# Later transposes, stores and inverse in the second block of a two-layer H3/MLP kernel, and row statistics moved in its last units

## The chip, the cores and the metric

The kernel runs on 1 core of a Trainium2 chip. The metric is device time in microseconds (us) from one launch, median of several runs; lower is better. In the tables PE is TensorE, DVE is VectorE, ACT is ScalarE, POOL is GpSimd, and SP is SyncE, whose queue issues all the DMAs of this kernel.

## What is computed

Sequence 2048 tokens, model width 1024, hidden width 3584, float32. Two layers, each of a convolution part A and an MLP part B, with the same weights in both layers:

```python
def A(q, k, v, shift_k, ssm_k, ssm_D):
    kv = causal_conv4(k, shift_k) * v                 # per channel, 4 taps
    y = causal_conv_2048(kv, ssm_k) + kv * ssm_D      # per channel, long
    return q * y
def B(x):
    return square(relu(x @ w1 + b1)) @ w2 + b2

x = q
x = x + A(layernorm(x), ...);  x = x + B(layernorm(x))
x = x + A(layernorm(x), ...);  x = x + B(layernorm(x))
```

The long convolution does not depend on x, so it is computed once (as transforms, products and inverse transforms) and used in both layers.

## The kernel before

**Units and steps.** The tokens are cut into four blocks of 512. A unit is the MLP of one layer on one block. `ORDER` lists the eight units as (layer, block): (0,0), (1,0), (0,1), (0,2), (1,1), (0,3), (1,2), (1,3). Each unit is a list of steps; one step multiplies with one 128x1024 or 512-wide slice of `w1` (kind `m1`) or `w2` (`m2`). All of it runs in a split form: each operand is a high part plus a low part, and `mm3` (L334 to L337) issues three matmuls for each product. A full `m1` or `m2` step is 12 matmuls. Units 5, 6 and 7 (`WINO`) use a seven-product scheme for the second matrix: their steps are `m1` (12 matmuls) and `w2` (6 matmuls), in four chunks; the first two chunks are 12 `m1` steps and 21 `w2` steps each, so the second chunk's `w2` steps are steps 45 to 65 of a unit of 154. Unit 0 has a special end: its last chunk's `m2` steps (106 to 133) and unit 1's first `m1` steps (134 to 157) handle half of the tokens each, so that the next unit's input can be made between them; a step there is half as long.

**Weights.** `w_advance` runs ahead of the step: it issues loads up to 8 weights ahead on SP's queue (`w_load`), ACT makes the high part (L1012), DVE or POOL the low part (L1020). The low part of a weight is put into DVE's queue three steps before it is used. Some weights are reloaded already split (`whl<-wd_m`, L1010).

**The convolution** goes on beside the MLP steps. Block 0's is made in a prologue. For the blocks sb = 1 to 3 two generators run, `fwd_x` (transforms of k and v, 8 groups of 128 channels for each block) and `fwd_g` (transforms of the filter). A call of `next` on both is an advance. The main loop gives them `FWD_RATE` advances a step (1.4 in units 0 to 2, none in half steps), and one more for a step in which the product generator `prod_stream` has nothing to do. `yield` ends what one advance does, so the number of yields sets how far apart two instructions stand in the program. `fwd_x` computes the shifted product on DVE (L365, L367), waits some advances, transposes it on TensorE (`transposes`, L420), multiplies with the transform tables (L391), adds and subtracts on DVE and stores to `XD` (L412). `fwd_g` loads filter rows and a carried part `KD` (L427, L436), multiplies (L454), copies (L459), stores the next carried part `KD` (L463), combines on DVE (L464 to L484) and stores `GD` (L493). Both use two PSUM banks `pt`, taken with `hold` or `take` and returned with `give`.

`prod_stream` loads `XD` and `GD` (L625), multiplies on POOL (L525), reduces on DVE (L529) and, through a list of delayed calls `lag`, runs `fin`: fold and butterfly on POOL (L675, L679), then for sb <= `PLAIN` = 1 `fin_plain`: inverse transform on TensorE (L595), copy on ACT (L601), store (L606). Its speed is `pace[u]`, the work of blocks 1 and 2 divided by the steps of units 0 to 2 (324.4 after a deduction) less `PACE_SLACK[1]`. In half steps the pace is a tenth.

**Row statistics.** `prep_a` makes the layernorm statistics of the next unit's input: it loads four 128x1024 row tiles `px` (L725; the pool has two buffers), runs two `bn_stats` (L696) and one `bn_aggr` (L697) on DVE for each, three steps apart, then the reciprocal root. It starts at step 28 of a unit, and what it makes is used from the step with 90 left. In `WINO` units `b2` is loaded at step 33 into the same pool `px` (L1737) and added to eight accumulator tiles on POOL from step 37 on (`add_b2w`, L1599).

Each engine and SP's queue work in program order.

Of the kernel before, what the change touches and what calls it, by code (L numbers as in the profile page):

```python
# [22 lines left out]
NB = S // T  # L23
# [4 lines left out]
BL = 256  # L28
NBL = S // BL
BT = T // BL  # L30
# [14 lines left out]
AHEAD_0 = 4  # L45
BURST = 1.06
FIN = "GGG"
PACE_SLACK = {1: 74, 3: 10}
PACE_TO = {1: 2}
PLAIN = 1  # L50
FILL = (16, 12, 8)
# [189 lines left out]
def tile_h3_mlp(ctx: ExitStack, tc: tile.TileContext, q, kT, vT, shk, ssmT, ssmD, w1, b1, w2, b2,  # L241
# [111 lines left out]
    def fwd_x(sb, c):  # L353
        k4 = mkfx([P, T + 3])
        SY.dma_start(k4, kT[c * P:(c + 1) * P, sb * T:sb * T + T + 3])
        v4 = mkfx([P, T])
        SY.dma_start(v4, vT[c * P:(c + 1) * P, sb * T:(sb + 1) * T])
        for _ in range(FWD_WAIT):
            yield
        ks = mkfx([P, T])  # L360
        w = shkt[:, c]
        A.activation(ks, k4[:, 3:], AF.Copy, scale=w[:, 0:1])
        yield
        for s in range(1, 4):
            V.scalar_tensor_tensor(ks, k4[:, 3 - s:T + 3 - s], w[:, s:s + 1], ks, op0=OP.mult, op1=OP.add)  # L365
        yield
        V.tensor_mul(ks, ks, v4)  # L367
        for _ in range(4 if sb == 1 else 7):
            yield
        o, = yield from hold(1)  # L370
        transposes(o, ks)
        yield
        if sb <= PLAIN:
            xt = mkfx([P, T])
            A.copy(xt, o)
        else:
            hi = mkfx([P, T], F32R)
            lo = mkfx([P, T], F32R)
            A.copy(hi, o)
            yield  # L380
            V.tensor_sub(lo, o, hi.bitcast(F32))
        yield
        give(o)
        yield
        oa = yield from hold(2)
        for e in range(2):
            for r in range(2):
                q_ = slice(e * 256, e * 256 + 256)
                ou = oa[e][:, r * 256:r * 256 + 256]
                if sb <= PLAIN:  # L390
                    PE.matmul(ou, plain[0][:, 2 * e + r], xt[:, q_], start=True, stop=True)  # L391
                else:
                    mm3(ou, fh[:, 2 * e + r], fl[:, 2 * e + r], hi[:, q_], lo[:, q_], True, True)
        yield
        odd = mkfx([P, T])
        A.copy(odd, oa[1])
        yield
        xo = cv.tile([P, 2, T], F32, name="fy", bufs=1)
        xv = xo.rearrange("p r (n u c) -> p u (r n) c", u=2, c=CG)
        ev = oa[0].rearrange("p (n c) -> p n c", c=CG)  # L400
        ov = odd.rearrange("p (n c) -> p n c", c=CG)
        V.tensor_add(xv[:, 0], ev, ov)
        V.tensor_sub(xv[:, 1], ev, ov)
        yield
        give(*oa)
        x2 = mkfx([P, T])
        V.tensor_add(x2, xo[:, 0], xo[:, 1])
        yield
        yield
        for i in range(3):  # L410
            t = x2 if i == 2 else xo[:, i]
            SY.dma_start(dview(XD[i], sb, c), t.rearrange("p (g b u) -> p g b u", g=2, b=BT))  # L412
        yield
# [15 lines left out]
    def fwd_g(sb, c):  # L429
        yield  # L430
        yield
        raw = mkfg([P, T])
        load_g(raw, sb, c)
        kk = [mkfk([P, 3 * BL]) for _ in range(2)]
        for r in range(2):
            SY.dma_start(kk[r][:, 0:BL], KD[sb - 1][c][:, r])  # L436
        for _ in range(FWD_WAIT):
            yield
        if sb > PLAIN:
            hi = mkfg([P, T], F32R)  # L440
            lo = mkfg([P, T], F32R)
            A.copy(hi, raw)
            yield
            V.tensor_sub(lo, raw, hi.bitcast(F32))
            yield
            yield
            yield
        oa = yield from hold(2)
        for r in range(2):
            ob = oa[r].rearrange("p (b e c) -> p e b c", b=BT, e=2)  # L450
            for e in range(2):
                q_ = slice(e * 256, e * 256 + 256)
                if sb <= PLAIN:
                    PE.matmul(ob[:, e], plain[0][:, 2 * e + r], raw[:, q_], start=True, stop=True)  # L454
                else:
                    mm3(ob[:, e], fh[:, 2 * e + r], fl[:, 2 * e + r], hi[:, q_], lo[:, q_], True, True)
        yield
        for r in range(2):
            A.copy(kk[r][:, BL:], oa[r])  # L459
        yield  # L460
        if sb < NB - 1:
            for r in range(2):
                SY.dma_start(KD[sb][c][:, r], kk[r][:, BT * BL:])  # L463
        V.scalar_tensor_tensor(kk[1][:, 0:T], kk[1][:, 0:T], sgn[:, 1:2], oa[0], op0=OP.mult, op1=OP.add)  # L464
        V.scalar_tensor_tensor(oa[1], kk[0][:, 0:T], sgn[:, 0:1], oa[1], op0=OP.mult, op1=OP.add)
        yield
        k0 = kk[1][:, 0:T]
        V.scalar_tensor_tensor(oa[0], oa[1], -1.0, k0, op0=OP.mult, op1=OP.subtract)
        V.tensor_sub(oa[1], oa[1], k0)
        yield  # L470
        odd = mkfg([P, T])
        parts = [t.rearrange("p (b e n) -> p e b n", b=BT, e=2) for t in (k0, oa[1], oa[0])]
        odds = [parts[0][:, 1]]
        for i in range(2):
            odds.append(odd[:, i * BL:i * BL + BL].rearrange("p (b n) -> p b n", b=BT))
            A.copy(odds[-1], parts[i + 1][:, 1])
        yield
        go = [None] * 3
        for i in (1, 2, 0):
            go[i] = mkfg([P, T])  # L480
            u = go[i].rearrange("p (g b u c) -> p u b g c", g=2, b=BT, u=2)
            ev, ov = (t.rearrange("p b (g c) -> p b g c", g=2) for t in (parts[i][:, 0], odds[i]))
            V.tensor_add(u[:, 0], ev, ov)
            V.tensor_sub(u[:, 1], ev, ov)  # L484
            yield
        if sb <= PLAIN:
            yield
            yield
        give(*oa)
        yield  # L490
        yield
        for i in range(3):
            SY.dma_start(dview(GD[i], sb, c), go[i].rearrange("p (g b u) -> p g b u", g=2, b=BT))  # L493
        yield
# [24 lines left out]
    def prod_stream():  # L519
# [11 lines left out]
        def fin(st, sm, sb, g, k):  # L531
# [4 lines left out]
                lag.at(1, fin, st, sm, sb, g, 1)  # L536
            elif k == 1 and sb <= PLAIN:
                st["z"] = butterfly(E, s)
                lag.at(2, fin_plain, st, sb, g, 0)
            elif k == 1:  # L540
                pair = st["pair"]
                if "l" not in pair if g % 2 else inv[1] < inv[0]:
# [1235 lines left out]
    for s, (k, u, c, a, i, tts, w) in enumerate(steps):  # L1778
# [109 lines left out]
            early.append(load_y(b, HALF[0]))  # L1888
        if u + 1 < NU and not direct[u]:
            n = s - start_step[u]  # L1890
            if n == 28:
                pa = prep_a(*ORDER[u + 1])
            elif n > 28 and pa is not None and next(pa, 0) == 0:
                pa = None
            if u in WINO and left == W_PREP:
                nxt = prep_w(*ORDER[u + 1], lag)
            elif u not in WINO and left == 18:
                while pa is not None:
                    if next(pa, 0) == 0:
                        pa = None  # L1900
                close_conv(ORDER[u + 1][1])
                nxt = prep_b(*ORDER[u + 1], lag)
# [77 lines left out]
```

## Time and profile before

| | |
|---|---|
| median of 3 runs | 2731.35 us (2731.30 to 2731.46) |
| the profiled execution | 2731.19 us |
| its span, first to last instruction | 2729.4 us |
| PE busy | 2683.3 us (98%) |
| DVE busy | 1989.7 us (73%) |
| ACT busy | 1124.2 us (41%) |
| POOL busy | 843.9 us (31%) |
| mean granted TensorE clock | 0.998 of full speed |

Busy time is the union of an engine's instructions. PE's instructions are pipelined and overlap, so what matters is the time in which PE has none, and the distance between the starts of two matmuls.

### The profile page before, as it was taken

To read this page: it belongs to the slowest core of one execution; us is meant where nothing else is said; L and a number is where in the kernel's file an instruction comes from. 1 tells how busy PE (TensorE), PEld (TensorE's weight loads), DVE (VectorE), ACT (ScalarE), POOL (GpSimd) and SP (SyncE) were. 2 spreads that over 40 slices of the span, in tenths; PEclk is the share of its full clock that TensorE was granted. 3 is DMA by queue.
4 is the path that set the end of the run, shared out by engine and by line. 5 is a ranking of instruction groups with operands and counts; after the bars stand their busy time and mean duration, and the time that the engine had idled before them with its cause. 6 is when DMAs were issued, how large, how long until landed. Compare 5 with 4: busy or idle time off the path is not lost.

```text
span 2729.4 us, 36532 instructions
## 1 busy us (share of the span) xinstructions
PE 2683.3 (98%) x12568; PEld 2228.9 (82%) x12568; DVE 1989.7 (73%) x3066; ACT 1124.2 (41%) x1936; POOL 843.9 (31%) x532
## 2 busy tenths in 40 slices
PE   7999999999999999999999999999999999999999
PEld 6888787888888888888888888888788788888887
DVE  7878888788987877779677665366787666664555
ACT  4454344433444233442234422244455444445443
POOL 2336565345532655236543454000100010001000
PEclk9999999999999999999999999999999999999999
DMA  8789898699989898888977887688888866676545
GB/s 253 262 301 316 285 312 285 221 312 369 324 298 324 295 338 280 267 332 284 349 263 269 301 295 253 226 288 311 300 284 295 281 229 211 229 276 200 178 166 204
DMA packets 377482, 755.05 MB, mean 277 GB/s; under 512 B 43840, under 2 KB 159184, under 8 KB 377296
## 3 DMA queue, kind: packets, MB, share of 16 engines
q1 hardware_dynamic: 377296, 752.72, 80.6%
q8 instruction: 99, 1.62, 0.2%
q14 instruction: 87, 0.71, 0.1%
HBM read 602.63 MB, written 149.95 MB: 276 GB/s over the span
## 4 chain that ended last, share of the span: by engine, by line
PE 84%; DVE 6%; DMA 5%; issue 1%; POOL 1%; ACT 1%; SPq 1%; DVEq 0%; ACTq 0%; POOLq 0%
PE p L336 26%; PE p L335 26%; PE p L337 26%; DMA wr<-w 2%; PE p L1095 2%; DVE whl L1020 1%; PE pt L335 1%; PE pt L337 1%; PE pt L336 1%; DMA whl<-wd_m 1%; DVE sm L529 0%; DMA cx<-xd 0%; PE pt L391 0%; DMA cg<-gd 0%; PE p L789 0%
## 5 line engine op out<-in xcount | busy, mean ns | idle before, releaser
L525 POOL TENSOR_TENSOR cp<-cx,cg 128x384 f32<-128x384 f32 (+5 forms) x288 | 541.8, 1893 | 580.3 <-DVE sm L529 388.1
L335 PE MATMUL p<-xh,whl 128*128 128x512 f32 (+1 forms) x1840 | 706.6, 384 | 3.3 <-DMA whl<-wd_m 2.5
L337 PE MATMUL p<-xh,whl 128*128 128x512 f32 (+1 forms) x1840 | 703.6, 382 | 3.6 <-DVE whl L1020 2.8
L336 PE MATMUL p<-xl,whl 128*128 128x512 f32 (+1 forms) x1840 | 702.8, 382 | 0.1
L1012 ACT CAST whl<-wr 128x512 fp32r<-128x512 f32 x637 | 383.5, 619 | 441.6 <-PE p L337 262.4
L1020 DVE TENSOR_TENSOR whl<-wr,whl 128x512 fp32r<-128x512 f32 x622 | 500.4, 825 | 78.4 <-ACT whl L1012 73.2
L335 PE MATMUL p<-whl,rh 128*128 128x512 f32 x1372 | 548.1, 399 | 3.7 <-ACT whl L1012 2.4
L336 PE MATMUL p<-whl,rh 128*128 128x512 f32 x1372 | 543.7, 396 | 1.9 <-POOL whl L1020 1.7
L337 PE MATMUL p<-whl,rl 128*128 128x512 f32 x1372 | 542.6, 396 | 0.0
L337 PEld LDWEIGHTS p<-xh,whl 128*128 128x128 f32 x1840 | 345.9, 188 | 71.7 <-DVE whl L1020 3.0
L335 PEld LDWEIGHTS p<-xh,whl 128*128 128x128 f32 x1840 | 346.2, 188 | 70.5 <-DMA whl<-wd_m 2.6
L336 PEld LDWEIGHTS p<-xl,whl 128*128 128x128 f32 x1840 | 346.0, 188 | 66.1 <-DVE xl L1408 0.3
L335 PEld LDWEIGHTS p<-whl,rh 128*128 128x128 f32 x1372 | 259.5, 189 | 64.0 <-ACT whl L1012 3.9
L336 PEld LDWEIGHTS p<-whl,rh 128*128 128x128 f32 x1372 | 259.5, 189 | 61.9 <-POOL whl L1020 2.6
L337 PEld LDWEIGHTS p<-whl,rl 128*128 128x128 f32 x1372 | 259.4, 189 | 60.6
L1502 DVE TENSOR_TENSOR rl<-wr,rh 128x512 fp32r<-128x512 f32 x140 | 141.1, 1009 | 182.8 <-ACT rh L1497 182.7
L1599 POOL TENSOR_TENSOR acc<-acc,px 128x512 f32<-128x512 f32 x18 | 23.1, 1317 | 771.0 <-DMA px<-b 771.0
L529 DVE TENSOR_REDUCE sm<-cp 128x128 f32<-128x384 f32 (+5 forms) x288 | 249.3, 874 | 9.2 <-POOL cp L525 9.2
L1494 ACT ACTIVATE wr<-p,b1t 128x512 f32<-128x512 f32 x138 | 95.2, 690 | 379.1 <-PE p L337 375.3
L1563 DVE TENSOR_TENSOR rl<-wr,rh 128x256 fp32r<-128x256 f32 x84 | 49.8, 593 | 208.5 <-ACT rh L1558 208.4
L1622 DVE TENSOR_TENSOR acc<-p,acc 128x512 f32<-128x512 f32 x152 | 101.5, 687 | 87.3 <-PE p L337 86.9
L1555 ACT ACTIVATE wr<-p,b1t 128x512 f32<-128x512 f32 x84 | 57.9, 689 | 190.4 <-PE p L337 188.9
(277 smaller groups left out, 3310.9 us busy)
## 6 DMA issues: line engine op xcount, KB each, us to landing
whl<-wd_m SPq DMA_DIRECT2D x379, 512.0 KB, 5.1
wr<-w SPq DMA_DIRECT2D x493, 256.0 KB, 5.4
wr<-td SPq DMA_DIRECT2D x152, 256.0 KB, 4.1
wd_m<-whl SPq DMA_DIRECT2D x70, 512.0 KB, 6.0
cx<-xd SPq DMA_DIRECT2D x48, 512.0 KB, 5.7
cg<-gd SPq DMA_DIRECT2D x48, 512.0 KB, 6.4
gd<-fg SPq DMA_DIRECT2D x72, 256.0 KB, 6.2
cx<-xd SPq DMA_DIRECT2D x48, 384.0 KB, 5.8
```

Source lines behind the costliest of these rows:

```text
L335: PE.matmul(o, lh, rh, start=start, stop=False)
L336: PE.matmul(o, lh, rl, start=False, stop=False)
L337: PE.matmul(o, ll, rh, start=False, stop=stop)
L525: G.tensor_mul(pr.rearrange("p c i -> p i c"), xt[:, 0:j + 1], gt[:, j::-1])
L529: V.tensor_reduce(sm[:, ty, jj], st["pr"], axis=AX.X, op=OP.add)
L1012: A.copy(t[:, 0], raws[n]["t"])
L1020: ENG[e[n % len(e)]].tensor_sub(t[:, 1], raws[n]["t"], t[:, 0].bitcast(F32))
L1095: PE.matmul(o, lh, r, start=start, stop=stop)
L1494: A.activation(r, st["o"], AF.Relu, bias=b1t[:, st["f"]:st["f"] + 1])
L1502: V.tensor_sub(st["lo"], st["r"]["t"], st["hi"].bitcast(F32))
L1555: A.activation(r, st["o"], AF.Relu, bias=b1t[:, st["f"]:st["f"] + 1])
L1622: V.tensor_add(accs[tt][:, d], o, accs[tt][:, d])
```

## The change

Five edits. (1) `fwd_x`: for block 1 the transposes come 7 advances after the product instead of 4, as for the other blocks. (2) `fwd_g`: the store of `KD` moves from right behind the copies to behind the return of the PSUM banks; the store of `GD` comes 4 advances later than that return for block 1 instead of 2 (2 still for the other blocks). (3) The inverse of block 1 is called 3 instead of 2 ticks of `lag` after the butterfly. (4) `PACE_SLACK[1]` is 76 instead of 74. (5) In units 5 and 6 `prep_a` starts at step 45 instead of 28.

```diff
-PACE_SLACK = {1: 74, 3: 10}
+PACE_SLACK = {1: 76, 3: 10}
...
         V.tensor_mul(ks, ks, v4)
-        for _ in range(4 if sb == 1 else 7):
+        for _ in range(7):
             yield
         o, = yield from hold(1)
         transposes(o, ks)
...
             A.copy(kk[r][:, BL:], oa[r])
         yield
-        if sb < NB - 1:
-            for r in range(2):
-                SY.dma_start(KD[sb][c][:, r], kk[r][:, BT * BL:])
...
         give(*oa)
-        yield
-        yield
+        if sb < NB - 1:
+            for r in range(2):
+                SY.dma_start(KD[sb][c][:, r], kk[r][:, BT * BL:])
+        for _ in range(4 if sb <= PLAIN else 2):
+            yield
         for i in range(3):
             SY.dma_start(dview(GD[i], sb, c), go[i].rearrange("p (g b u) -> p g b u", g=2, b=BT))
...
                 st["z"] = butterfly(E, s)
-                lag.at(2, fin_plain, st, sb, g, 0)
+                lag.at(3, fin_plain, st, sb, g, 0)
...
             n = s - start_step[u]
-            if n == 28:
+            at = 45 if u in WINO else 28
+            if n == at:
                 pa = prep_a(*ORDER[u + 1])
-            elif n > 28 and pa is not None and next(pa, 0) == 0:
+            elif n > at and pa is not None and next(pa, 0) == 0:
                 pa = None
```

## Rows read from the trace of the kernel before

**Rows 1.** The page, part 1: busy us, share of the span, instructions.
```profile
PE 2683.3 (98%) x12568; PEld 2228.9 (82%) x12568; DVE 1989.7 (73%) x3066; ACT 1124.2 (41%) x1936; POOL 843.9 (31%) x532
```
**Rows 2.** Waits of PE: us in total, times, longest.
```profile
PE p L420 <- DVE fx L1134: 13.5, 3, 9.4
PE pt L420 <- DVE fx L367: 6.9, 3, 6.0
PE p L335 <- DMA whl<-wd_m: 3.6, 4, 2.2
...
PE pt L595 <- DVE fg L484: 2.0, 1, 2.0
```
**Rows 3.** Windows: length; PE, PEld, DVE, ACT, POOL busy; clock; DMA.
```profile
294.00:306.00 12.00, 5.97 (x21) 4.83 (x20) 11.66 (x16) 1.51 (x4) 8.42 (x8) 0.72 0.87 268
...
440.00:470.00 30.00, 25.89 (x114) 20.74 (x113) 22.82 (x35) 13.65 (x24) 15.49 (x11) 0.94 0.75 242
470.00:546.00 76.00, 70.83 (x460) 63.08 (x459) 59.20 (x105) 35.70 (x60) 26.05 (x17) 1.00 0.67 239
546.00:820.00 274.00, 272.63 (x1294) 227.51 (x1294) 236.51 (x320) 111.72 (x202) 137.08 (x85) 1.00 0.94 325
```
**Rows 4.** Timeline of DVE, 276 to 304 us: start, length, instruction.
```profile
291.96 0.41 DVE L484 TENSOR_TENSOR fg<-pt,fg 128x256 f32<-128x256 f32 x1
...
297.03 1.49 DVE L484 TENSOR_TENSOR fg<-fk 128x256 f32<-128x256 f32 x1
298.44 1.48 DVE L1020 TENSOR_TENSOR whl<-wr,whl 128x512 fp32r<-128x512 f32 x1
299.84 0.68 DVE L367 TENSOR_TENSOR fx<-fx 128x512 f32<-128x512 f32 x1
```
**Rows 5.** Timeline of PE, 292 to 307 us.
```profile
304.55 0.63 PE L336 MATMUL p<-whl,rh 128*128 128x512 f32 x1
304.97 0.63 PE L337 MATMUL p<-whl,rl 128*128 128x512 f32 x1
```
**Rows 6.** Waits of SP's queue, whole span: us, times, longest.
```profile
SPq L493 <- DVE fg L484: 36.6, 13, 8.8
...
SPq L463 <- ACT fk L459: 19.4, 11, 6.9
...
SPq L725 <- POOL fk L1599: 18.4, 2, 9.6
```
**Rows 7.** Timeline of SP, 438 to 475 us.
```profile
450.06 1.44 SPq L493 DMA_DIRECT2D gd<-fg  x3
...
460.74 1.52 SPq L1004 DMA_DIRECT2D wr<-w  x3
```
**Rows 8.** Timeline of DVE in unit 5, 1890 to 1930 us.
```profile
1902.77 1.29 DVE L696 BATCH_NORM_STATS2 st<-px 128x6 f32<-128x512 f32 x2 [0.43 <-DMA px<-x]
...
1904.21 1.24 DVE L1606 TENSOR_TENSOR acc<-p,acc 128x512 f32<-128x512 f32 x2
```
**Rows 9.** Timeline of DVE in unit 5, 1936 to 1972 us.
```profile
1960.32 1.39 DVE L1606 TENSOR_TENSOR fx<-p,fx 128x512 f32<-128x512 f32 x2 [0.23 <-PE p L337]
1961.63 0.68 DVE L1020 TENSOR_TENSOR whl<-wr,whl 128x512 fp32r<-128x512 f32 x1
```
**Rows 10.** Timeline of DVE in unit 6, 2238 to 2268 us.
```profile
2251.56 1.39 DVE L1606 TENSOR_TENSOR fx<-p,fx 128x512 f32<-128x512 f32 x2 [0.62 <-PE p L337]
...
2255.78 1.39 DVE L1606 TENSOR_TENSOR fx<-p,fx 128x512 f32<-128x512 f32 x2 [1.03 <-PE p L337]
2257.09 1.89 DVE L1020 TENSOR_TENSOR whl<-wr,whl 128x512 fp32r<-128x512 f32 x3
```
**Rows 11.** Timeline of PE, unit 5, step 63 of the unit.
```profile
1965.04 0.39 PE L335 MATMUL p<-whl,cg 128*128 128x512 f32 x1
1965.27 0.40 PE L336 MATMUL p<-whl,cg 128*128 128x512 f32 x1
```
**Rows 12.** Timeline of PE, unit 6, step 63 of the unit.
```profile
2260.73 0.40 PE L336 MATMUL p<-whl,cg 128*128 128x512 f32 x1
```

## The prediction

> **What bounds the kernel now.** I read the page first: PE is busy 2683.3 us of 2729.4 and the next engine, DVE, 1989.7 [rows 1]. So PE sets the time, and a change that leaves its matmuls as they are, as this one does, can win or lose only the 46 us in which PE has nothing, and what a lowered clock costs behind a long gap. Next, who PE waits for [rows 2]. The 13.5 us for L1134 are the prologue, which no edit touches. Within reach are the transposes of `fwd_x` waiting for DVE's product (L367): 6.9 us in three waits, one of them 6.0; the inverse (L595) waiting for a bank that DVE still reads: 2.0; and reloaded weights (`whl<-wd_m`): 3.6, the longest 2.2. Third, the windows, to see where the gaps lie [rows 3]: 294 to 306 us has 6.0 idle and a granted clock of 0.72; 440 to 470 has 4.1 idle and 0.94; the half steps, 470 to 546, have 5.2 idle; the 274 us behind them only 1.4, although DVE is busy 236.5 of them. Last, the queues: SP stood 36.6 us for the stores of `GD`, 19.4 for those of `KD`, and 18.4, in two waits of up to 9.6, before a load of `px` for POOL's addition of `b2` [rows 6].
>
> **The transposes (edit 1).** At 294.6 PE came to the transposes, and DVE executed the product they need at 299.84 to 300.5 [rows 4]: the 6.0 us. The next 12 matmuls then stood 0.42 us apart [rows 5] where a full-clock pair is 0.23 apart [rows 11]; that is the clock's lower level, 1.2 GHz, after 6 us without work, and costs 12 x 0.19 = 2.3. With the other two waits (0.9) this edit has 9.2 us to win. It will not win all. Three more advances at 1.4 a step are about two steps, 2 x 12 x 0.23 = 5.5 us. Instead of waiting, PE would do two steps first, and the second needs the low part of a weight that DVE made at 298.44 to 299.92, just before the product [rows 4]. PE would ask for it at 294.6 + 2.8 + 0.2 = 297.6, so 2.3 us of the wait go over to the weight. I take 9.2 - 2.3 = **-6.9**; bounds 0 (DVE later still) and -9.2.
>
> **What moves with it.** A group of `fwd_x` now takes 3 more advances, one of `fwd_g` 2. Over eight groups that is up to 24 advances, at 1.4 a step 17 steps (48 us); advances given while the product generator is idle make it fewer. The work is the same, only stretched, so DVE is less dense up to step 106 and what is left is done after the half steps, at the same rates; there DVE is already at 86% with 1.4 us idle on PE [rows 3], so I cost it at nothing, and at 2 us (another wait of the size of L595's) as the upper bound. Since alignments of DVE, ACT and SP all shift, I put those **+2** into the sum for a new wait somewhere in units 0 and 1.
>
> **The stores (edit 2).** SP's waits cost PE nothing while weights are ahead. At one place they do: SP stood up to 8.8 us until 450.06 for a `GD` store and had a backlog until 460.74, when it came back to the weights [rows 6, 7]; PE then ran dry in the window 440 to 470, which holds 4.1 idle, the inverse's 2.0 among them, and about 2 more at the lower clock (0.94) [rows 3]. The store is one of block 2's first group, for which the delay stays 2 advances; but that group now comes some 10 to 17 steps later, where the half steps stop the streams. So this stall of 6.1 either goes or turns up elsewhere: I take half, **-3**; bounds 0 and -6.1. The other `KD` and `GD` waits are hidden by weights loaded up to 8 steps ahead, and moving them wins nothing.
>
> **Inverse and pace (edits 3, 4).** The wait of L595 is in the stall just counted; other inverses never waited, so one tick more is nothing unless the product generator, which lets two groups be open, idles for it: it then hands its turn to the transforms. The pace rises by 2/248, 0.8%: nothing.
>
> **The row statistics (edit 5).** In unit 5 SP stood at the third `px` load until POOL had added `b2`; it could not issue the reloaded weights queued behind, and PE waited 2.2 us [rows 2, 6], with the restart 2.3. In unit 6 SP waited 9.6 and PE not at all. With `prep_a` at step 45, `b2` has left `px` before the tiles are asked for, so **-2.3**. But where does DVE now do it? From `bn_stats` to the next instruction one tile takes 1904.21 - 1902.77 = 1.44 [rows 8], four take 5.8. Before, they stood among `m1` steps, many of whose weights come already split. Now they stand behind steps 49, 52, 55 and 58, in a stretch of `w2` steps of 6 x 0.23 = 1.4 us, each of which needs a low part (0.6) from DVE, and evictions besides. At step 63 of unit 5 the low part was done at 1962.31 and needed at 1965.27 [rows 9, 11]: 2.96 ahead. All four tiles stand before it: 5.76, less 0.23 that DVE idled [rows 9], less 2.96, leaves **+2.6** on PE. In unit 6 the same part was done at 2257.77 and needed at 2260.73 [rows 10, 12], 2.96 again, with 0.62 + 1.03 idle on DVE ahead of it: 5.76 - 1.65 - 2.96 = **+1.15**. No other step of the stretch comes out worse. The bounds: nothing, if DVE's queue has more slack than its order shows, to the whole 5.8 in each unit. The four loads of `px` now share the queue with the `w2` weights; at worst that is once more a wait for a weight of 2.2 [rows 2], and I take nothing, since these weights are asked for 8 steps ahead. Edit 5 comes to **+1.5**.
>
> **Sum.** 2731.2 (this execution: span and 1.8 around it) - 6.9 - 3 + 2 + 1.5 = 2724.8; the median of the runs is 0.2 above the execution: **2725**.
>
> A rule that speaks against edit 1: the Trainium skill, page "SBUF — State Buffer", section "Who interferes with whom", says that a DVE instruction with two SBUF inputs and a GpSimd instruction that reads SBUF exclude each other for a whole instruction. The trace agrees: L484 took 1.49 us from SBUF alone and 0.41 with one input in PSUM [rows 4]. By that rule DVE's lateness comes from POOL's products and goes with them, and the sum would be that of the first rival.
>
> **Rivals.**
> *The wait only changes hands.* DVE is late at 294 us because its instructions took two to three times as long (1.48 for a low part against 0.68 at other places [rows 4, 9]) while POOL was busy 8.4 of 12 us [rows 3]. If POOL's products and this lateness come again beside each later transposes, PE waits for weights instead: half of 6.9 is won, the stall at 440 to 470 is replaced, and -3.4 + 2 + 1.5 gives 2731. For it: the low part stands right before the product in DVE's queue. Against: less is asked of DVE in each step before the half steps.
> *Everything clears.* -9.2 - 6.1 - 2.3, no new wait, statistics hidden: 2714. For it: DVE's waits on its own inputs leave holes. Against: the 2.96 us of lead.
> *The streams are caught at step 106 (slower).* There the program takes both `pt` banks, and makes advances on the spot until they are free. If `fwd_x` then stands between its product and its matmuls, these follow with no steps between them: a wait like the one removed, 8.3 with the clock, and one of 2.0 for a copy. -6.9 + 10.3 + 2 + 1.5 = +6.9: 2738. It decides if the generator holds or wants banks just then; before, block 2's first group already stood there, and 24 advances shift what stands there by an unknown part of a group of 22.
>
> **How the numbers follow.** No change, as far as this kernel can be measured, is within 0.2%, 5.5 us: 2725.9 to 2736.8. The forecast has 0.62, the first rival 0.17, the second 0.10, the third 0.11. The forecast's own range, from its bounds, is 2719 to 2730; seven tenths of it lie below 2725.9. Faster: 0.43 + 0.10 = 0.53. Same: 0.19 and the first rival, 0.36. Slower: 0.11. The range 2714.5 to 2733 takes in the first rival and most of the second and leaves out the third.
>
> **What would show it.** In the changed profile: PE's wait at L420 for L367 below 1 us in all, and in its place up to 2.3 for `whl` L1020; no window before 440 us with a clock near 0.7; the long stand of SP for L493 no longer within 20 us of the half steps; PE's wait for `whl<-wd_m` in unit 5 gone and SP's for L725 on POOL too; in units 5 and 6, in the second chunk's `w2` steps, PE waiting for L1020, 2.6 and 1.2 us. The prediction is wrong if L420 still waits, if half steps lose more than 8 us, or if the statistics cost nothing or more than 6.

## The result, and the profile after

The changed kernel takes **2744.6 us** (median of 6 runs, 2739.9 to 2747.0), the kernel before 2731.3 beside it (6 runs): ratio 1.0046, 95% interval 1.0033 to 1.0059. It is slower by 0.46%. I had forecast 2725, range 2714.5 to 2733. The profiled execution took 2744.4 (before 2731.2), its span 2742.6 (before 2729.4).

The page of the kernel after, part 1, against [rows 1]:
```profile
PE 2689.8 (98%) x12568; PEld 2229.5 (81%) x12568; DVE 1980.7 (72%) x3066; ACT 1124.6 (41%) x1936; POOL 835.4 (30%) x532
```
PE's time without work grew from 46.1 to 52.8 us, half of the 13.2, and the same 12568 matmuls keep PE busy 6.5 us longer. About half of these 6.5 is the clock: by the clock records of the two traces it stood at its lower level, 1.2 GHz, for 17.1 us in all instead of 10.2, which at half speed costs about 3.4 us (an estimate). Where the rest lies was not traced. What PE waits for in the kernel after (total, times, longest), against [rows 2]:
```profile
PE p L336 <- DVE whl L1020: 8.8, 10, 3.8
PE p L335 <- DMA whl<-wd_m: 6.2, 5, 3.7
PE pt L336 <- DVE yl L561: 3.0, 2, 2.0
```
The 6.9 us for L367 have no row any more; nor has L595. In their place stand low parts that DVE makes, those of weights (L1020) and of the inverse's input (L561). Waits for reloaded weights (`whl<-wd_m`) have grown from 3.6 [rows 2]. Windows of the kernel after (length; PE, PEld, DVE, ACT, POOL busy; clock; DMA), against [rows 3]:
```profile
294.00:306.00 12.00, 12.00 (x57) 9.89 (x56) 11.61 (x18) 3.63 (x7) 7.75 (x7) 1.00 1.04 387
306.00:440.00 134.00, 134.00 (x625) 111.75 (x624) 115.80 (x171) 61.27 (x111) 81.03 (x65) 1.00 0.88 290
440.00:470.00 30.00, 24.53 (x99) 18.58 (x98) 28.17 (x36) 9.99 (x17) 17.07 (x14) 0.94 0.95 351
...
546.00:820.00 274.00, 268.52 (x1260) 222.46 (x1259) 235.15 (x321) 109.16 (x199) 127.82 (x81) 0.99 0.93 322
640.00:650.00 10.00, 6.96 (x29) 5.44 (x28) 10.00 (x12) 1.83 (x3) 5.67 (x3) 0.84 1.05 355
915.00:930.00 15.00, 11.32 (x38) 8.71 (x37) 15.00 (x21) 2.59 (x5) 7.22 (x5) 0.77 1.03 345
```
From 294 to 440 us PE has no idle time left, more than I hoped for. Behind it PE is idle in places that were full: 5.5 us in 546 to 820, where it was 1.4, with the clock at 0.84 of full speed in one stretch and 0.77 in a later one. DVE is busy for 235.2 us of that window, as much as before (236.5 [rows 3]). The kernel after is 16 us ahead at 440 us, so a window there holds later steps than the same window of the kernel before.

Steps can be found in both traces by their first matmul, so each program step's start tells where time comes and goes. Steps are counted through the whole program: 106 is the first half step of unit 0, 594 begins unit 5, 639 is that unit's step 45. Differences to the kernel before, in the profiled executions (the last column is the ratio of the runs to those of the kernel before beside them, with its 95% interval):

| kernel | ahead (-) at step 106 | 106 to 594 | 594 to 639 | 639 to end | span | ratio of runs |
|---|---|---|---|---|---|---|
| after | -16.0 | +25.5 | -2.6 | +6.3 | +13.2 | 1.0046 [1.0033, 1.0059] |
| e1: edit 5 alone | -0.4 | +1.5 | -2.6 | +4.3 | +2.8 | 1.0005 [0.9996, 1.0014] |
| e2: after without edit 5 | -16.0 | +21.4 | +4.1 | +1.3 | +10.8 | 1.0048 [1.0031, 1.0065] |
| e3: edit 1 alone | -11.9 | +34.8 | -0.2 | +0.9 | +23.7 | 1.0085 [1.0070, 1.0101] |
| e17: edit 2 alone | +0.1 | +33.5 | +0.3 | +1.5 | +35.4 | 1.0131 [1.0114, 1.0148] |
| e18: edit 3 alone | +0.9 | +9.4 | +0.0 | +0.6 | +11.0 | 1.0043 [1.0028, 1.0058] |
| e7: edit 4 alone | -1.9 | +4.8 | +4.0 | +0.8 | +7.7 | 1.0041 [1.0025, 1.0057] |
| e8: after without edit 1 | -9.7 | +25.7 | -2.6 | +6.2 | +19.6 | 1.0071 [1.0054, 1.0088] |
| e10: after without edit 4 | -16.0 | +31.4 | -2.6 | +5.4 | +18.2 | 1.0064 [1.0047, 1.0081] |

So the change wins 16.0 us before the half steps and gives back 25.5 in units 0 to 4 behind them; 3.7 are lost in the last units. In the kernel after the 25.5 lie at few places: steps 106 to 120 (4.1), 134 to 158 (3.0), 190 to 194 (8.0), 278 to 282 (6.7; a reloaded weight comes 3.7 us late at 921 us), the rest in smaller ones.

Two things have to be known to read these differences. First, they hold matmuls that moved as well as waits. At step 106 the kernel after has done 24 convolution matmuls fewer, about 2.8 us of work (an estimate from the distances of such matmuls, 0.11 to 0.12 us), so that much of the 16.0 is only put off and comes back in the 25.5. At steps 190 to 194 PE idles 3.0 us and the clock takes about 1.6 (0.84 over 10 us); most of the rest of the 8.0 is matmuls that stood in neighbouring steps before. Free of this is PE's time without work between steps 106 and 594: 8.9 us before, 23.1 after. Second, two executions of one program differ. After and e2 have the same program up to unit 5; PE idles 23.1 and 22.6 us in steps 106 to 594, but the clock was low for 17.1 and 6.8 us, and they lose 25.5 and 21.4. A difference of some 4 us in that column therefore says little.

### The profile page after: what moved, and what is told of

Read it like the earlier page. It is cut to its first block, busy times and chain, and to the rows that moved or that the text cites. A ratio compares the mean times of both kernels' runs of the same rounds, so it can differ in the third digit from the quotient of the medians.

```text
span 2742.6 us, 36481 instructions
## 1 busy us (share of the span) xinstructions
PE 2689.8 (98%) x12568; PEld 2229.5 (81%) x12568; DVE 1980.7 (72%) x3066; ACT 1124.6 (41%) x1936; POOL 835.4 (30%) x532
## 4 chain that ended last, share of the span: by engine, by line
PE 82%; DMA 7%; DVE 6%; issue 2%; POOL 1%; ACT 1%; SPq 1%; DVEq 0%; POOLq 0%; ACTq 0%
PE p L336 25%; PE p L335 25%; PE p L337 25%; DMA cg<-gd 2%; PE p L1095 1%; DMA wr<-w 1%; DVE whl L1020 1%; DMA whl<-wd_m 1%; PE pt L337 1%; PE pt L336 1%; PE pt L335 1%; POOL cp L525 1%; PE pt L454 0%; DMA wd_t<-whl 0%; PE p L789 0%
## 5 line engine op out<-in xcount | busy, mean ns | idle before, releaser
L525 POOL TENSOR_TENSOR cp<-cx,cg 128x384 f32<-128x384 f32 (+5 forms) x288 | 535.9, 1876 | 608.0 <-DVE sm L529 306.5
L1020 DVE TENSOR_TENSOR whl<-wr,whl 128x512 fp32r<-128x512 f32 x622 | 499.8, 824 | 62.5 <-ACT whl L1012 59.7
L529 DVE TENSOR_REDUCE sm<-cp 128x128 f32<-128x384 f32 (+5 forms) x288 | 250.3, 875 | 47.6 <-POOL cp L525 47.6
L1502 DVE TENSOR_TENSOR rl<-wr,rh 128x512 fp32r<-128x512 f32 x140 | 147.4, 1053 | 171.0 <-ACT rh L1497 170.8
L1599 POOL TENSOR_TENSOR acc<-acc,px 128x512 f32<-128x512 f32 x18 | 23.1, 1318 | 779.5 <-DMA px<-b 779.5
```

What stands on the lines that cost most here:

```text
L525: G.tensor_mul(pr.rearrange("p c i -> p i c"), xt[:, 0:j + 1], gt[:, j::-1])
L529: V.tensor_reduce(sm[:, ty, jj], st["pr"], axis=AX.X, op=OP.add)
L1020: ENG[e[n % len(e)]].tensor_sub(t[:, 1], raws[n]["t"], t[:, 0].bitcast(F32))
L1502: V.tensor_sub(st["lo"], st["r"]["t"], st["hi"].bitcast(F32))
```

## The experiments

**Which edit? Edit 5 alone (e1) and the rest without it (e2).** e1 is the kernel before with edit 5, e2 the kernel after without it.

> The kernel before with edit 5 alone (row statistics of units 5 and 6 start at step 45). Up to step 621 its program is the kernel before's. Theory A (the loss of the change lies before unit 5; edit 5 costs DVE time in the w2 steps): the 2.3 us wait for the reloaded weights in unit 5 goes, the w2 steps 45 to 65 get 4 us longer in unit 5 and 0.8 in unit 6: +2 to +3 us on the kernel before. Theory B (edit 5 is what makes the change slower): +10 or more.

> The changed kernel without edit 5 (edits 1 to 4 alone). Theory A: the changed kernel's time less 2.5, so about +10 us on the kernel before, with the same losses in units 1 and 2 (8 us at steps 190 to 194, 7 us at steps 278 to 282). Theory B: 0 to -5 us on the kernel before.

e1 took 2732.5, no change that can be measured; without edit 5 the rest loses as much as with it (e2: 2743.2). In e1's trace the wait of unit 5 goes (-2.45 in the unit's steps 39 to 41), 2.4 come back in the `w2` steps of unit 5 and 0.8 in those of unit 6. The loss lies in the edits to the convolution, as theory A expected of both runs (e1 is 1.4 us behind where it expected 2 to 3). Among the other edits, edit 5 even wins a little: behind step 594 the kernel after loses 3.7 and e2 5.4, in one execution each.

**Edit 1 alone (e3) and everything else (e8).** e3 is the kernel before with edit 1, e8 the kernel after without it.

> The kernel before with edit 1 alone (transposes 7 advances behind the product for block 1). Theory A (stretching the second block's transforms pushes products and transforms past step 106, where they collide): about 10 us won up to step 106 and most of it or more lost behind, +3 to +12 us in all. Theory C (the losses behind step 106 are accidents of how the streams fall against the steps, so each variant has its own): the win up to step 106 is there, the losses at steps 190 and 278 are not, and the total lies anywhere from -12 to +12.

> The changed kernel without edit 1 (transposes 4 advances behind the product; the stores, the inverse, the pace and the row statistics as changed). Theory A: fwd_g alone takes 21 advances instead of 19, so there is about two thirds of the lateness; the 6 us wait of the transposes stays or moves; +5 to +15 us on the kernel before. If edit 1 alone makes the lateness: within 5 us.

e3 took 2754.6, e8 2751.0. e3 wins 11.9 up to step 106 and then loses 34.8, more than all edits together. Without edit 1 the others lose 25.7 of their own in the same stretch. The edits don't add up: alone, edits 1 to 4 cost 23.7, 35.4, 11.0 and 7.7 of span. Both runs lie above every range I had given, e3 23.4 us and e8 17.0 behind the kernel before.

**The pace: alone (e7), taken back (e10), to the other side (e11).** e7 has `PACE_SLACK[1]` 76 in the kernel before, e11 has 72 there; e10 is the kernel after with 74.

> The kernel before with edit 4 alone (slack 76 instead of 74: products 0.8% faster in units 0 to 2). Theory A: nothing, within 3 us of the kernel before. Theory C (accidents of alignment make up the loss): a shift as small as this moves single waits by 5 us or more, and the total by up to 10 either way.

> The changed kernel with PACE_SLACK[1] back at 74, so edits 1, 2, 3 and 5 without the higher pace. The pace alone cost about 10 us in the medians when put into the kernel before (5.7 in its profiled execution up to the end of unit 2 and in unit 5). If the pace's loss is a cost of its own that adds: 2734 to 2738, and steps 190 to 282 lose less. Theory C (no cost adds, each order has losses of its own): its losses stand at other steps than those of the changed kernel, with a total that can't be told from the parts, 2735 to 2760; at steps 106 it is still 14 to 16 us ahead of the kernel before, because edit 1 has acted there already.

> The kernel before with PACE_SLACK[1] 72 instead of 74: the pace of the products 0.8% lower instead of 0.8% higher, nothing else. If a higher pace costs because DVE and POOL get more work in each step, a lower pace costs nothing or wins: 2729 to 2732. Theory C (74 is matched to the rest of the order, so a step to either side loses): slower, 2735 to 2750, with new waits of 2 to 4 us of PE for DVE's low parts or for reloaded weights at single places of units 0 to 2.

0.8% more pace costs 0.41% (e7: 2744.1), 0.8% less costs 0.39% (e11: 2742.2, ratio 1.0039 [1.0024, 1.0054]), and with the old pace the kernel after is no better (2748.8). It isn't the load that a higher pace brings, since a lower one costs as much. The value 74 fits this order of the program, and a step to either side costs some 10 us. All three runs are as theory C, that the order is matched as a whole, expected.

**Are the streams late at step 106, and is that the cause? (e4, e5, e6)** In the kernel after, 83 products are done when step 106 begins, in the kernel before 90 (counted from L525's instructions), and seven more go through in the first half steps. e4 is the kernel after, with the products in half steps held to a tenth of the pace even when they are behind; e5 the kernel after with `FWD_RATE` 1.6 for unit 0, which brings the transforms back to where they were; e6 the kernel before with 1.2, which delays them.
```diff
-FWD_RATE = {0: 1.4, 1: 1.4, 2: 1.4, 3: 1.1, 4: 1.1, 5: 1}
+FWD_RATE = {0: 1.6, 1: 1.4, 2: 1.4, 3: 1.1, 4: 1.1, 5: 1}
```


> The changed kernel, with products in the half steps held to a tenth of the pace even when the product stream is in arrears (in the changed kernel arrears let through one product at nearly each half step: 7 in steps 106 to 120 where the kernel before had 1). Theory A: the 4 us that steps 106 to 120 lose go, and the products are made after step 158 instead, 2738 to 2743 in all, with the losses at steps 190 and 278 as before or larger. Theory C: the losses behind step 158 change their place and size, so that the total may lie anywhere from -10 to +15 on the kernel before.

> The changed kernel with 1.6 advances a step in unit 0 instead of 1.4, which makes up for the longer generators (22 advances a group instead of 19). Theory A (what is lost behind step 106 is lost because fewer transforms and products are done before it): the number of products at step 106 is again near 90, block 2's first transposes come before step 106, the losses at steps 106 to 120, 190 and 278 shrink; about -10 us on the kernel before. Theory C (accidents of alignment): the products at step 106 rise too, but there are losses of 5 to 10 us somewhere in units 1 and 2 all the same; anywhere from -10 to +15.

> The kernel before with 1.2 advances a step in unit 0 instead of 1.4: the second block's transforms come as late as in the changed kernel, but no distance between two instructions changes. Theory A: the loss of the changed kernel without its win, +15 to +30 us. If the longer distances, not the lateness, cost behind step 106: within 5 us of the kernel before.

e4 took 2740.6 (1.0030 [1.0017, 1.0043]): steps 106 to 120 lose 0.9 instead of 4.1, but 20.7 are lost up to step 594. e5 took 2761.0 (1.0107 [1.0092, 1.0123]), although it had 86 products done at step 106; e6 2767.6 (1.0130 [1.0115, 1.0145]). e4 is where either theory put it. e6 agrees with theory A (33.6 us behind, for 15 to 30 expected), but a lower rate also changes which instructions meet, so it doesn't show that lateness by itself costs. e5 was to win 10 us by theory A and loses 27, more than theory C allowed: making up for most of the lateness doesn't help. My first theory, that the work pushed behind step 106 is the whole cause, falls.

**Repair one wait where it stands (e9).** At 644 us PE waits 2.0 for the inverse's low part and drops to the lower clock. e9 is the kernel after with
```diff
                 if g % 2:
-                    lag.at(1, fin, st, sm, sb, g, 4)
+                    lag.at(2, fin, st, sm, sb, g, 4)
```


> The changed kernel, with the inverse transforms of blocks 2 and 3 called 2 ticks behind the low part yl instead of 1; nothing else. In the changed kernel PE waits 3.0 us in two waits for yl, one of 2.0 at 644 us, and steps 190 to 194 take 8.0 us longer than before. Theory A2 (each loss is PE meeting, in program order, an instruction whose input DVE makes just ahead of it; it can be repaired where it stands): the wait and most of the 8.0 go, steps 190 to 194 lose at most 2, and about 6 of it is left at the end: 2738. Theory C (the order of the kernel before is matched as a whole; each repair shifts what comes behind): steps 190 to 194 lose at most 2 as well, but other losses of 2 to 8 us come up in steps 194 to 594, and the end is within 3 us of the changed kernel, 2742 to 2748, or above.

e9 took 2751.9 (1.0075 [1.0060, 1.0090]). It is slower still, as theory C expected in total, and steps 190 to 194 lose 8.4 instead of 8.0, where both theories had them repaired. Waits of PE in e9, and the matmul at the place:
```profile
PE pt L336 <- DVE fx L381: 4.5, 1, 4.5
```
```profile
645.28 0.58 PE L336 MATMUL pt<-fx,fh 128*128 128x256 f32 x1 [4.51 <-DVE fx L381]
```
The inverse is out of the way, so PE comes to the next instruction that needs DVE, a transform, and waits 4.5 there. DVE itself is late, whatever asks for it. Why it is late is seen in the timelines of DVE and of POOL in the kernel after, 632 to 652 us (start, length):
```profile
634.14 2.34 DVE L1020 TENSOR_TENSOR whl<-wr,whl 128x512 fp32r<-128x512 f32 x1
...
638.27 2.04 DVE L1020 TENSOR_TENSOR whl<-wr,whl 128x512 fp32r<-128x512 f32 x1
...
643.23 3.00 DVE L561 TENSOR_TENSOR yl<-sm,yh 128x256 fp32r<-128x256 f32 x2
646.15 0.68 DVE L381 TENSOR_TENSOR fx<-pt,fx 128x512 fp32r<-128x512 f32 x1
646.76 0.68 DVE L1020 TENSOR_TENSOR whl<-wr,whl 128x512 fp32r<-128x512 f32 x1
```
```profile
633.89 2.04 POOL L525 TENSOR_TENSOR cp<-cx,cg 128x768 f32<-128x768 f32 x1
...
638.18 3.85 POOL L525 TENSOR_TENSOR cp<-cx,cg 128x640 f32<-128x640 f32 x2
642.33 3.63 POOL L525 TENSOR_TENSOR cp<-cx,cg 128x640 f32<-128x640 f32 x2 [0.29 <-DMA cg<-gd]
650.73 1.79 POOL L525 TENSOR_TENSOR cp<-cx,cg 128x640 f32<-128x640 f32 x1 [4.78 <-DMA cg<-gd]
```
The same low part of a weight takes 2.34 and 2.04 while POOL multiplies and 0.68 as soon as POOL pauses at 646. Over the whole trace of the kernel before, the 494 low parts of DVE with no POOL instruction beside them took 0.68 each (longest 0.69); the 128 that overlap one took 1.37 in the mean, up to 2.90 (worked out from all instructions of L1020 on DVE and of POOL).

**Take POOL's products away, or DVE's sums (e13 to e16).** Two pairs, each of the kernel before and the kernel after with the same part of the computation left out. In e13 and e14 POOL multiplies one column of each product, and DVE sums as many elements as ever, that column repeated:
```diff
-            pr = cv.tile([P, CU, j + 1], F32, name="cp", bufs=3)
-            G.tensor_mul(pr.rearrange("p c i -> p i c"), xt[:, 0:j + 1], gt[:, j::-1])
-            st["pr"] = pr
+            pr = cv.tile([P, CU, 1], F32, name="cp", bufs=3)
+            G.tensor_mul(pr.rearrange("p c i -> p i c"), xt[:, 0:1], gt[:, j:j + 1])
+            st["pr"] = pr.to_broadcast([P, CU, j + 1])
```
In e15 and e16 POOL's products are whole and DVE sums one column:
```diff
-            V.tensor_reduce(sm[:, ty, jj], st["pr"], axis=AX.X, op=OP.add)
+            V.tensor_reduce(sm[:, ty, jj], st["pr"][:, :, 0:1], axis=AX.X, op=OP.add)
```


> The kernel before with POOL's products left out but for one column of each (288 instructions of about 1.8 us become short ones); DVE sums the same number of elements as before, from that one column repeated, so the convolution's values are not computed. Program order, transforms, loads and stores are those of the kernel before. Theory D (POOL beside DVE makes DVE late): DVE's low parts (L1020) fall from up to 2 to 3 us to 0.7, the wait of 6.0 us for the product of the transform (L367) at 294 us goes with its slow clock (8.3), as does most of the stall at 440 to 470: 2714 to 2722. Theory C (order alone): the waits at 294 and 440 us stay where they are: 2727 to 2732.

> The changed kernel with the same part of the products left out. Theory D: none of the losses behind step 106 is left but those of the row statistics, so it comes within 3 us of the kernel before with light products, 2714 to 2724. Theory C: it stays 8 us or more behind the kernel before with light products, with waits of PE at steps 190 to 194 and 278 to 282 still there: 2735 or more.

> The kernel before with DVE's sums of the products left out but for one column of each (288 reductions of about 0.9 us, 250 us of DVE in all, become short ones); POOL's products stay, so the convolution's values are not computed. Theory D: DVE has slack but its two-input instructions stay long beside POOL; most of the waits go, 2716 to 2726. If only POOL's interference matters and not DVE's load, the wait at 294 us stays, 2727 to 2731. Theory C: 2727 to 2732.

> The changed kernel with the same part of the sums left out. Theory D: within 3 us of the kernel before with light sums, or ahead of it by what the first edit wins, 2714 to 2727. Theory C: 8 us or more behind that kernel, 2736 or more.

| pair | before, median | after, median | after over before: at 106 | 106 to 594 | behind 594 | span |
|---|---|---|---|---|---|---|
| whole kernels | 2731.3 | 2744.6 | -16.0 | +25.5 | +3.7 | +13.2 |
| e13, e14: POOL light | 2719.6 | 2726.4 | -6.1 | +6.4 | +6.4 | +6.7 |
| e15, e16: sums light | 2728.8 | 2743.3 | -10.4 | +24.7 | +4.0 | +18.3 |

PE's time without work in steps 106 to 594 is 8.9 and 23.1 us in the whole kernels, 8.5 and 10.0 with POOL light, 7.7 and 23.0 with the sums light.

Page, part 1, of e14 and of e16, the two changed kernels:
```profile
PE 2682.0 (99%) x12568; PEld 2225.4 (82%) x12568; DVE 1807.6 (66%) x3066; ACT 1125.0 (41%) x1936; POOL 457.4 (17%) x532
```
```profile
PE 2690.9 (98%) x12568; PEld 2230.7 (81%) x12568; DVE 1835.2 (67%) x3066; ACT 1125.9 (41%) x1936; POOL 830.1 (30%) x532
```
DVE is relieved by about the same in both, 173 and 146 us. Where POOL still multiplies, the loss behind step 106 is whole (24.7); where it doesn't, three quarters of it are gone (6.4 of 25.5 left), and the changed kernel is level with its partner when unit 5 begins (+0.3). So it isn't how much DVE has to do, it is POOL's products. Theory D is borne out for them, though not in full: e14 is 6.8 us behind e13, where it expected at most 3 and theory C 8 or more. For the sums it was wrong: e16 is where theory C put it. e14's DVE at the place where the kernel after lost 8.0:
```profile
628.68 0.82 DVE L529 TENSOR_REDUCE sm<-cp 128x128 f32<-128x640 f32 x1 [0.36 <-POOL cp L525]
629.42 0.75 DVE L561 TENSOR_TENSOR yl<-sm,yh 128x256 fp32r<-128x256 f32 x2
630.08 0.68 DVE L381 TENSOR_TENSOR fx<-pt,fx 128x512 fp32r<-128x512 f32 x1
630.68 0.68 DVE L1020 TENSOR_TENSOR whl<-wr,whl 128x512 fp32r<-128x512 f32 x1
```
The two halves of `yl` take 0.75 together instead of 3.00, and PE does not wait for them. e13 also shows that the larger part of the wait of 6.0 us that edit 1 was meant for hangs on POOL's products: in the same program order it is 2.4 in e13 (292.6 to 295.0 us), and the clock does not fall, where it was 0.72 [rows 3]. The window of the stall at 440 us is fuller too. Windows of e13, which is 6 us ahead of the kernel before at the first and 11 at the second:
```profile
294.00:306.00 12.00, 10.98 (x54) 9.37 (x55) 9.59 (x17) 3.49 (x7) 4.94 (x7) 1.00 0.99 313
...
440.00:470.00 30.00, 27.65 (x121) 21.78 (x121) 19.59 (x32) 12.39 (x22) 3.89 (x5) 1.00 0.98 333
```
Left over are 6.4 of the 25.5. About 2.8 of them are the matmuls put off at step 106, and the wait of 3.8 us in step 116 of the kernel after is still 2.8 in e14, so that place has another cause as well.

Why does the order of the kernel before meet so few waits? Its low parts are not shorter (1.25 us in the mean in steps 158 to 194, 0.99 in the kernel after). The traces give a part of the answer. DVE works in program order, and between steps 106 and 594 of the kernel before it never stands at a sum (L529) for a product that POOL has not made. In the kernel after it stands there for 23.1 us, in 11 waits of up to 8.5, and the low parts queued behind the sum stand with it. This standing alone is not the loss: e14 has 22.9 us of it, in 12 waits of up to 5.1, and e18 loses 9.4 without it. That DVE comes late from such a stand and then can't catch up, because its instructions are long beside POOL, is argued from these numbers and not tested by itself. Nor does the pair part the length of DVE's instructions from POOL's products being made sooner.

**The stores alone (e17) and the inverse alone (e18).** e17 is the kernel before with edit 2, e18 the kernel before with edit 3.

> The kernel before with edit 2 alone: the stores of KD behind the return of the banks, those of GD two advances later for block 1. fwd_g of block 1 gets 2 advances longer for each group, so it too is pushed behind step 106, less than by edit 1. By the prediction: the stall at 440 to 470 us loses half, 2728. Theory D (any shift of the streams makes low parts late beside POOL's products): a few us ahead at step 106 at most, then 5 to 20 lost between steps 106 and 594: 2735 to 2750.

> The kernel before with edit 3 alone: the inverse transforms of block 1 one tick later. It moves single instructions of PE, ACT and SP by a step or less and no transform. By the prediction nothing: 2731, within 2. Theory D as well, unless the product generator idles for it and gives its turn to the transforms; then 5 to 15 lost behind step 106 as in the other variants: 2736 to 2746.

The stores alone took 2766.1, the dearest of all edits and above the 2750 that I had allowed; the inverse took 2741.2, within what I had allowed. e18 shows the pattern in small: it is 8.0 ahead at step 60 (the wait for L367 at 294 us has moved) and 0.9 behind at step 106, because the same wait is met at 300 us with 4.0 and L595 waits 3.4:
```profile
PE pt L420 <- DVE fx L367: 6.1, 3, 4.0
PE pt L595 <- DVE fg L484: 3.4, 1, 3.4
```

**b2 behind the statistics (e12).** This is an attempt at what edit 5 wanted, without bn_stats among `w2` steps. It also moves `b2` in unit 7. e12 is the kernel before with
```diff
-                lag.at(34, load_b2, bst)
-                lag.at(38, add_b2w, bst, wacc)
+                lag.at(44, load_b2, bst)
+                lag.at(48, add_b2w, bst, wacc)
...
-            if n == 28:
+            at = 33 if u in WINO else 28
+            if n == at:
...
-            elif n > 28 and pa is not None and next(pa, 0) == 0:
+            elif n > at and pa is not None and next(pa, 0) == 0:
```


> The kernel before with b2 and the row statistics in the other order: in units 5 and 6 the statistics start at step 33 instead of 28, so that they fall among the second chunk's m1 steps, and b2 is loaded ten steps later, behind them (step 43 instead of 33, added from step 47 instead of 37). Units 0 to 4 are the same. If my account of edit 5 holds (the wait of 2.45 us for a reloaded weight at step 39 of unit 5 comes from SP standing behind the px load, and the 2.4 us it gives back come from bn_stats among w2 steps), this order has neither: 2.4 us faster in unit 5 and nothing lost in unit 6, 2728 to 2729. Rival: POOL's eight additions now lie beside DVE's low parts in the w2 steps and slow them as elsewhere (0.68 to 1.5 us), PE waits 2 to 4 us in each unit, 2731 to 2736.

e12 took 2749.1 (1.0064 [1.0049, 1.0079]). The 2.45 of unit 5 are won, as expected. Then the `w2` steps lose 8.1 in unit 5 and 8.2 in unit 6, and unit 7 loses 3.5: it is the rival, at twice its price, and outside both ranges. Timelines of e12, of POOL, DVE and PE:
```profile
1938.26 8.45 POOL L1599 TENSOR_TENSOR acc<-acc,px 128x512 f32<-128x512 f32 x6 [230.65 <-DMA px<-b]
```
```profile
1941.26 1.51 DVE L1568 TENSOR_TENSOR yl<-wr 128x256 f32<-128x256 f32 x1
1942.81 1.38 DVE L1569 TENSOR_TENSOR yl<-yl,wr 128x256 f32<-128x256 f32 x1
1944.11 1.48 DVE L1570 TENSOR_TENSOR yl<-wr 128x256 f32<-128x256 f32 x1
1945.51 1.48 DVE L1571 TENSOR_TENSOR yl<-wr,yl 128x256 f32<-128x256 f32 x1
1946.91 1.75 DVE L1020 TENSOR_TENSOR whl<-wr,whl 128x512 fp32r<-128x512 f32 x1
```
```profile
1948.72 0.79 PE L336 MATMUL p<-whl,rh 128*128 128x512 f32 x1 [5.21 <-DVE whl L1020]
1949.31 0.63 PE L337 MATMUL p<-whl,rl 128*128 128x512 f32 x1
1949.74 0.63 PE L335 MATMUL p<-whl,rh 128*128 128x512 f32 x1
```
Four instructions that are 0.42 each at other places stand 1.4 apart beside POOL's addition, the low part behind them comes 5.2 late, and PE goes on at 0.43 a matmul, the level of 1.2 GHz (granted clock 0.50 from 1948 to 1954 us). Here nothing of the convolution is involved: one POOL job moved by ten steps does it.

No variant that computes everything beats the kernel before; e1 equals it.

## Why the prediction was wrong

**The step that failed is "What moves with it"**: the work that edits 1 and 2 push behind step 106 is done "after the half steps, at the same rates", and "I cost it at nothing". Steps 106 to 594 cost 25.5 us, about 2.8 of it matmuls put off from before and the rest waits and the lower clock: PE stands 23.1 us there instead of 8.9. I had the two numbers that speak against it in the same sentence, DVE at 86% and PE idle 1.4 us of 274 [rows 3], and read the small idle time as cover. It said only that in this one order hardly a low part came late. DVE's rate did stay the same, 235.2 us of 274, and PE waited all the same.

The rule I quoted, the Trainium skill, page "SBUF — State Buffer", section "Who interferes with whom", bears on why a shift is dear. It says that a DVE instruction with two SBUF inputs contends with a GpSimd instruction that reads SBUF, over ports that are an exclusive lock; that the lock is held for a whole instruction it says of DVE's two-port modes. The runs agree as far as they go, 0.68 against 1.37 us for L1020, and 19 of the 25.5 gone without POOL's products. I had used it for edit 1's wait alone and not for the work that moves.

None of the three signs that I had named for a wrong prediction came: L420 waits no more, steps 106 to 158 lose 7.0 us (the limit was 8), and the statistics cost 1.7 us (e1) to 3.7 by the traces (nothing, or more than 6, was to be the sign). They did not look at steps 158 to 594, where 18.4 us were lost. The range was also too narrow for its own terms: "2719 to 2730", given as from the bounds, is not their sum, which reaches to some 2743.

**Inverse and pace, "nothing"**: wrong by the same reasoning. Alone they cost 11.0 and 7.7 of span.

**The stores, -3**: the stall did go, and about as much came back a few steps on. In the kernel before PE waits 2.0 us in step 102 for the inverse's bank and 1.9 in step 111 for the high part of a weight, which ACT makes from a load that SP issued at 460.74, after its backlog [rows 7]. Waits of PE in the kernel before, 440 to 546 us:
```profile
PE p L335 <- ACT whl L1012: 2.4, 2, 1.9
PE pt L595 <- DVE fg L484: 2.0, 1, 2.0
```
In the kernel after SP's wait for `GD` is down from 36.6 with a longest of 8.8 [rows 6] to this row (line 493 is the same store there):
```profile
SPq L493 <- DVE fg L481: 13.6, 11, 3.3
```
Neither of PE's two waits is left. In 440 to 480 us it waits for low parts instead, 3.8 of it in step 116:
```profile
PE p L336 <- DVE whl L1020: 5.5, 4, 3.8
```
So of "either goes or turns up elsewhere" the second came, and steps 106 to 120 lose 4.1. e13 parts the stall. POOL is light there and SP's long stand is as before (8.4 us). The wait for the bank is gone, and the one for the weight, the longest in this row of e13, is still 1.7:
```profile
PE p L335 <- ACT whl L1012: 2.5, 2, 1.7
```
So POOL's products made one half of the stall, and SP's backlog, as the prediction read it, is left for the other. That edit 2 is what removes it is not shown: e3, with the stores where they were, has neither wait in steps 102 and 111.

**The transposes, -6.9**: right in mechanism, and near in size. L367 vanished from PE's waits, and nothing took its place at 297.6 (the 2.3 us that I had handed on to the weight). The kernel after is 16.0 ahead at step 106, but that is not edit 1's alone: the other edits are 9.7 ahead there without it (e8), so it adds 6.3, and alone it wins 11.9 (e3), above my bound of 9.2. Edits 2 and 3 alone are 7.1 and 8.0 ahead at step 60 as well and lose it again by step 106. It was all given back.

**The new wait, +2**: a guess of one wait; there were four places, of 3 to 8 us each with its clock and the matmuls that moved there.

**Edit 5, +1.5**: near. e1 shows -2.45, +2.4 and +0.8, +1.7 in all behind step 633 for a forecast of -2.3, +2.6 and +1.15; in the kernel after unit 5 takes 4.0 instead of 2.6, and 3.7 are lost in all. At e1's runs, 1.0005 [0.9996, 1.0014], the sum can't be told from nothing.

**The rivals.** The first (2731) named what e13 and e14 bear out, POOL beside DVE with PE waiting for weights instead, but expected it beside the transposes and priced it at half of their 6.9. The slower one (2738) had the right sign and a place near the first loss, but not the mechanism: no transposes stood waiting at step 106, and those steps lost 4.1, not 10.3. Of the two causes that I held against each other on the way, lateness of the streams and a program order that fits its constants, neither is the whole: the order decides, and POOL's products set most of the price of leaving it.

## What to carry to other kernels

Here the engine that sets the time had almost no idle time in a stretch where another was at 86%, and each of the twelve variants that shift the convolution and compute everything was slower, whatever it was meant to do. In such a kernel a term "moved, same work, costs nothing" should be bounded by a whole stretch of new waits. In steps 106 to 594 these were 5 to 9 us for 0.8% of pace or one tick, and 33 to 35 for two or three advances. Measure such a kernel's sensitivity first, by one constant moved a little to both sides, before crediting an edit with the wait that it removes. And before moving a POOL job, read which DVE instructions will lie beside it, and with what lead the bound engine needs them. When two traces are compared at the place of a wait, compare the same program steps, not the same time.

## What the runs showed of the hardware that was not expected

A DVE instruction of 128x256 with two inputs in SBUF takes 0.42 us alone and 1.4 to 1.5 beside POOL (e12; L561 in the kernel after), more than three times; one of 128x512 goes from 0.68 up to 2.9. Busy time doesn't tell what this is worth. Leaving out nearly half of POOL's busy time (461.3 of 843.9 us remain), on an engine busy for 31% of the span, takes 0.37% from the kernel before (e13: 0.9963 [0.9950, 0.9976]); leaving out 150 us of DVE's own work takes 0.09% (e15: 0.9991 [0.9981, 1.0000]).
